# Attention and two mixture-of-experts layers on one core: closer choice steps, two lists in line, turns in two pieces, tile-by-tile reuse, early rows from 36 tiles

## The chip, the cores and the metric

The kernel runs on one core of a Trainium2 chip. The metric is the device time of one execution in microseconds. Times are given in us throughout. The core's engines are named as the profile names them: PE (TensorE, matrix products), PEld (its weight loads), DVE (VectorE), ACT (ScalarE), POOL (GpSimd) and SP (SyncE, which here issues transfers and runs no arithmetic).

## The reference

Three steps follow one another, each on the output of the one before:

```python
# 1 attention, B=8 batches, H=8 heads, S=576 positions, 64 per head
ret = (0.125 * q @ k.T * Dmat) @ v            # Dmat[i,j] = gamma_h**(i-j) for i>=j, else 0
x = ret as 4608 rows of 512
# 2 first mixture: each row goes to its best of 8 experts
e = argmax(x @ w_gate);  gate = softmax(x @ w_gate)[e]
x = gate * (relu(x @ w1[e]) @ w2[e])          # w1: 512x1024, w2: 1024x512
# 3 second mixture: greedy, each expert takes at most 576 rows
logits = x @ w_gate2
for (row, e) in order of falling logits:
    if row is free and e holds under 576 rows: assigned[row] = e
out = relu(x @ w1b[assigned]) @ w2b[assigned]
```

## The kernel before

**Attention** handles 36 tiles of 128 rows. For each tile a row of stages runs (list `stages`, in `step`), each some steps off the others. The stage `split` makes the gate's two f16 halves of the transposed row tile: ACT rounds `xT` to `xTh`, and POOL subtracts (`xTl = xT - xTh`, 128x512). PE multiplies both with the gate weights. Near the end of attention, some tiles of rows that are already stored in DRAM (`Xs`) are gathered by POOL for the first expert.

**The first mixture (moe1)** runs its experts e = 0 to 7 one after another. Every f32 product is made of three f16 products (high by high, high by low, low by high). An expert has a first layer (PE line L568 into PSUM `ph`; ACT makes `hh` from it at L573, DVE `hl` at L574) and a second layer (L590, L594 into `py`). Weights arrive in f32 `stage` buffers by SP transfers (L428), ACT rounds them (L449) and DVE takes the difference (L452). The rows of the next experts are gathered by POOL (L485), scaled by ACT and DVE and turned by transposing transfers of SP (L526, into `xT`). Where in a layer's groups of matmuls these side jobs are emitted is written out by hand in dictionaries `steps` and `at`, whose keys count matmul groups: `N6` gives the places in e6's first layer at which parts of e7's rows are prepared. Expert 0 starts with SA = 3 row tiles, and the first layer for its last two is run later, with side jobs at its own `steps`. The output rows of moe1 are written to `X1s`, 40 tiles of slots (8 experts by 5 tiles): tiles 30 to 39 are those of e6 and e7. In e6's first layer `fill` (places 124, 134, ...) writes tiles of it by indirect transfers of POOL (L1054) to listed positions; the last `LATE` tiles are written by plain SP transfers.

**The second mixture (moe2)** takes one expert after another, in eight phases. For each phase `choose` finds which expert is next, which rows it takes and their list. It searches a threshold in R = 5 digits; a digit has the steps `cnt` (DVE compares the keys, `cmp`, L1502; PE counts, L1508), `any` (DVE L1511, L1513; PE L1516) and `dig` (DVE L1520; PE L1523; DVE L1526), and after the digits come `sum` (PE L1540) and the list: `base` (PE L1603) and `list` (PE L629, then DVE up to the indices `ix`, L638). In phases 0, 1 and 7 the list runs in line, right after `sum`; in phases 2 to 6 it is put in a queue `aside` and runs beside the next choice's digits. When the list is there, `prepare` puts jobs in a queue `tasks`: gathers of five row tiles by POOL (L485, `xg`), their transposes by SP (L526), and the weights' loads and splits.

The moe2 loop is paced by PE: `during` counts the columns of the matmuls emitted, at 2.4 GHz, in ns. When the counter `left` is used up, the next step of the choice is emitted; its length for each kind of step is in `FIRST` (choice 0), `SECOND` (choice 1) and `PACE` (from choice 2 on). `ASIDE` is the same for lists in the queue, and `GAP` for the tasks (2.7 us up to phase 1, then 3.8 us). Each engine then executes its instructions in the order emitted. Choice p+1 and its list thus run in the layers of phase p. On POOL, the gathers stand in line with indirect writes of the output (L1697). On SP, the weight loads stand in line with the transposes and with a load of the chosen expert's number (`es`, L1723).

Tiles come from pools: `fp`, `wp2`, `sp` and the PSUM pool `fps` are opened after attention (`open_ffn`), in the memory that attention's pools held. In their plain form, a tile's first use waits for all that used the earlier pool's memory.

Of the kernel before, what the change touches and what calls it, by code (L numbers as in the profile page):

```python
# [24 lines left out]
SA = 3  # L25
LEAD_IN = 6
CAST = (4, 3)
EARLY = ((28, 1), (29, 0), (29, 1), (30, 1), (32, 0), (32, 1), (33, 0), (33, 1), (34, 0), (34, 1), (35, 0))
LOADS_LAST = 29
T0 = (76, 88)  # L30
LATE = 3
SOON = 3
P0 = (1, 12, 24, 70, 84)
RANK = (32, 40, 48)
N1 = (14, 82, 102, 122, 142, 170)
LOGITS = (96, 99, 101, 105, 109)
N6 = (10, 50, 66, 82, 98, 114)
G6 = (4, 8, 40, 122, 139)
G7 = (30, 36, 70, 106, 140, 170)
R = 5  # L40
NONE = -1.0e30
LEAD = 2
PACE = dict(key=7000, cnt=3300, any=2200, dig=1900, sum=3600, base=4000, list=3000)
SECOND = dict(key=3600, cnt=2500, any=1700, dig=1500, sum=2600, base=3000, list=2600)
FIRST = dict(key=3000, cnt=1700, any=1200, dig=800, sum=1900, base=3400, list=2600)
ASIDE = dict(key=8500, base=5000, list=5000)
AFTER_FIRST = 7500
GAP = (2700, 3800)

# [84 lines left out]
def attention(k, q, kk_, v, wg1, consts, X, after, ahead):  # L134
    tc = k.tc
# [196 lines left out]
    def step(s, stages):  # L332
        if s == 2 - LEAD_IN:
            nc.sync.dma_start(G[:, 0], consts[:, NC:NC + 512].rearrange("p (h q) -> p h q", q=128))
            k.wg1 = split_gate(k, wg1, "wg1", True)
        for f, off in stages[1:] + stages[:1] if s == LOADS_LAST else stages:
            if f is None:
                store()
                if (s, off) in EARLY:
                    next(ahead, None)  # L340
            elif 0 <= s - off < NT:
                f(D[s - off])
        for g, at0, every in after:
            if s >= at0 and (s - at0) % every == 0:
                next(g, None)
# [125 lines left out]
def open_ffn(k):  # L471
    tc = k.tc
    k.fctx = ExitStack()
    k.fp = k.fctx.enter_context(tc.tile_pool(name="fp", bufs=2))
    k.wp2 = k.fctx.enter_context(tc.tile_pool(name="wp2", bufs=1))
    k.sp = k.fctx.enter_context(tc.tile_pool(name="sp", bufs=1))
    k.fps = k.fctx.enter_context(tc.tile_pool(name="fps", bufs=2, space=bass.MemoryType.PSUM))
    k.tp = lambda shape: k.fps.tile(shape, F32, name="tp")


# [477 lines left out]
def moe1(k, X, X1, w1, w2):  # L958
# [106 lines left out]
    for e in range(8):  # L1065
# [77 lines left out]
        if e < 6:  # L1143
            x1 = columns(e)
            for s in (4, 0, 1, 2, 3) if small(e) else range(5):
                at = {8: load}
                if s == SA and e == 0:
                    steps = {64: load, 40: lambda: next(p1, None)}
                    mixed(layer1(k, xTs[0], w, CAP1, to=hs[0], spans=[[(128 * SA, CAP1 - 128 * SA)]]), steps)
                if s == (3 if small(e) else 4) and e < 6:  # L1150
                    ahead = prep(e + 2)
                    at[4] = lambda: next(ahead, None)
                if s == 4 and small(e):
                    last = tail(e, mixed(layer2(k, hs[e], w, s, True), at), x1)
                    next(last)
                    continue
                if s == 0 and small(e):
                    at[12] = partial(next, last)
                if e == 0 and s < SA:
                    go = lambda: next(p1, None)  # L1160
                    at = ({4: load, 12: go, 18: load}, {4: load, 18: load}, {2: go, 14: go, 21: load})[s]
                if e == 0 and s >= SA:
                    at = {2: go, 12: load, **({6: at[4]} if 4 in at else {})}
                if e == 5 and s < 2:
                    at[18] = load
                last = second(e, s, mixed(layer2(k, hs[e], w, s), at), x1)
# [311 lines left out]
def choose(k, ph, es_out, ix_out, aside):  # L1478
# [84 lines left out]
        late(nc.vector.tensor_scalar(z[:, 0], f.rem, 0.0, -30000.0, op0=OP.is_le, op1=OP.mult))  # L1563
        late(nc.vector.tensor_tensor(f.nr, z[:, 0], f.rem, op=OP.subtract))

    if ph in (0, 1, 7):
        yield from listed(k, ph, z, z1, key, s8, ix_out)
        if ph < 7:
            onward()
    else:  # L1570
        onward()
        aside.append(listed(k, ph, z, z1, key, s8, ix_out))
# [128 lines left out]
def moe2(k, X1, w1, w2, out, rest):  # L1701
# [18 lines left out]
    def choices():  # L1720

        for ph in range(8):
            for t in choose(k, ph, lambda es: ev.setdefault(ph, nc.sync.value_load(es[0:1, 0:1], min_val=0, max_val=7)),  # L1723
                            lambda ix, ph=ph: lx.setdefault(ph, ix), aside):
                while t == "sum" and aside:
                    side()
                if t == "key":
                    state.side = ASIDE[t]
                yield AFTER_FIRST if ph == 1 and t == "key" else (FIRST, SECOND, PACE)[min(ph, 2)][t]

    choice = choices()

# [32 lines left out]
    def prepare():  # L1765

        n = state.ph + 1
        if n == 0:
            if 0 in ev and 0 not in weights:
                half(0, 1)  # L1770
        elif n in lx and n not in weights:
            half(n, 1)
            t = tasks[-5:]
            del tasks[-5:]
            r = [(True, partial(turned, n, s)) for s in range(5)]
            tasks.extend([(True, partial(fetched, n))] + t[:2] + r[:2] + t[2:3] + r[2:4] + t[3:4] + r[4:] + t[4:])
            half(n, 2)

    def due(first):
# [130 lines left out]
```

## Time and profile before

| | us |
|---|---|
| median of 3 runs (lowest, highest) | 1115.98 (1108.40, 1120.48) |
| the profiled execution, and its span | 1111.99, 1110.2 |
| PE busy | 1027.6 |
| DVE busy | 615.2 |
| ACT busy | 431.3 |
| POOL busy | 303.3 |
| attention | 0 to 205 |
| moe1 | 205 to 653 |
| moe2 phases 0 to 7 | 653 to 1110 |

The engines run unsynchronized, each through its own list; an engine's idle time before an instruction is put down to what released it. PE is the engine to watch, as it is busy for nearly the whole span: its idle times, and the stretches in which its granted clock is below 1.0 (full speed is 2.4 GHz), are where time can be had. In rows of a timeline the first number is the start in us, the second the length, then engine, line and operation, `out<-in`, shape and count; brackets hold the idle time before the instruction and its releaser.

### The profile page before, as it was taken

The numbers are of one execution on the slowest core, as the hardware profiler recorded it, in microseconds if no ns is written. First come the engines' busy times: TensorE is split into PE (matmuls) and PEld (weight loads), VectorE is DVE, ScalarE is ACT, GpSimd is POOL, SyncE is SP. The second block draws the span as 40 slices with busy tenths as digits, with TensorE's granted clock in tenths as the row PEclk, the third lists the DMA queues.
The fourth block names the chain that finished last, engine by engine and source line by source line (L and its number), as shares of the span: only waits on it lengthen the run. The fifth ranks groups of instructions, "written<-read, shape, count | busy, mean of one in ns | idle before, by whom it ended". The sixth has DMA issues, their size and how long they took to land.

```text
span 1110.2 us, 23634 instructions
## 1 busy us (share of the span) xinstructions
PE 1027.6 (93%) x9227; PEld 680.3 (61%) x9227; DVE 615.2 (55%) x1678; ACT 431.3 (39%) x817; POOL 303.3 (27%) x542
## 2 busy tenths in 40 slices
PE   7999998798999999999899989995968989799996
PEld 5887887456766757474675446653636565557572
DVE  3455565786866666475625756643636473625140
ACT  3445545365645545364521342312313131324230
POOL 5444444221230313120311232213040313224101
PEclk9999999999999999999999999997998999899999
DMA  9999996488777887889750444628264555567521
GB/s 193 210 226 237 232 233 162 134 228 197 199 206 162 213 175 192 171 214 243 156 96 21 145 129 119 168 76 190 77 127 121 144 145 122 170 156 182 141 65 43
DMA packets 307255, 178.17 MB, mean 160 GB/s; under 512 B 240448, under 2 KB 273984, under 8 KB 307136
## 3 DMA queue, kind: packets, MB, share of 16 engines
q1 hardware_dynamic: 296672, 144.25, 56.2%
q0 software_dynamic: 10464, 32.34, 9.4%
q8 instruction: 74, 1.21, 0.5%
q14 instruction: 45, 0.37, 0.1%
HBM read 117.09 MB, written 31.28 MB: 134 GB/s over the span
## 4 chain that ended last, share of the span: by engine, by line
PE 73%; DMA 8%; issue 6%; DVE 4%; SPq 3%; ACT 3%; POOL 2%; POOLq 0%; ACTq 0%; DVEq 0%
PE ph L568 30%; PE py L594 24%; PE tp L120 7%; PE pO L120 5%; PE pS L120 3%; PE py L590 2%; SPq L526 2%; DMA xg<-X1s,ix 1%; POOL xg L485 1%; DMA xT<-xg 1%; DMA X1s<-x1r 1%; SPq L120 1%; DMA xg<-Xs,ix 1%; DMA xT<-xhl 1%; DMA out_dram<-x1r,ti 1%
## 5 line engine op out<-in xcount | busy, mean ns | idle before, releaser
L568 PE MATMUL ph<-xT,w1h 128*128 128x288 f16 (+4 forms) x2048 | 367.4, 295 | 44.3 <-DMA xT<-xg 31.6
L568 PEld LDWEIGHTS <-w1h 128*128 128x128 f16 x2048 | 198.3, 99 | 109.0 <-issue 31.2
L568 PE MATMUL ph<-xT,w1l 128*128 128x288 f16 (+4 forms) x1024 | 230.0, 295 | 0.0
L594 PE MATMUL py<-w2h,hh 128*128 128x512 f16 x512 | 194.3, 379 | 0.0
L594 PE MATMUL py<-w2h,hl 128*128 128x512 f16 x512 | 194.2, 379 | 0.0
L594 PE MATMUL py<-w2l,hh 128*128 128x512 f16 x512 | 194.1, 379 | 0.0
L594 PEld LDWEIGHTS <-hh 128*128 128x128 f16 x1024 | 98.2, 98 | 109.1 <-issue 0.8
L573 ACT ACTIVATE hh<-ph 128x576 f16<-128x576 f32 (+4 forms) x136 | 81.9, 604 | 188.2 <-PE ph L568 181.7
L574 DVE SCALAR_TENSOR_TENSOR hl<-ph,hh 128x576 f16<-128x576 f32 (+4 forms) x136 | 95.0, 699 | 57.4 <-ACT hh L573 56.7
L568 PEld LDWEIGHTS <-w1l 128*128 128x128 f16 x1024 | 100.8, 99 | 30.5 <-issue 1.0
L452 DVE SCALAR_TENSOR_TENSOR w1l<-stage,w1h 128x1024 f16<-128x1024 f32 x60 | 72.8, 1222 | 61.5 <-ACT w1h L449 60.5
L594 PEld LDWEIGHTS <-hl 128*128 128x128 f16 x512 | 50.1, 98 | 56.9
L452 DVE SCALAR_TENSOR_TENSOR w2l<-stage,w2h 128x1024 f16<-128x1024 f32 x64 | 78.1, 1224 | 9.6 <-ACT w2h L449 8.5
L120 DVE TENSOR_TENSOR s<-pS,ct 128x512 f32<-128x512 f32 x72 | 46.3, 685 | 42.6 <-PE pS L120 42.6
L449 ACT ACTIVATE w1h<-stage 128x1024 f16<-128x1024 f32 x60 | 61.8, 1047 | 19.1 <-DMA stage<-in_moe_w_dram 19.1
L449 ACT ACTIVATE w2h<-stage 128x1024 f16<-128x1024 f32 x64 | 66.9, 1047 | 2.2 <-DMA stage<-in_moe_w_dram 2.2
L120 POOL TENSOR_TENSOR xTl<-xT,xTh 128x512 f16<-128x512 f32 x35 | 42.6, 1218 | 87.3 <-ACT xTh L120 87.3
L499 ACT ACTIVATE x1r<-py 128x512 bf16<-128x512 f32 x37 | 22.1, 596 | 97.0 <-PE py L594 78.1
L485 POOL DMA_INDIRECT xg<-X1s,ix x40 | 42.2, 1055 | 59.9 <-DVE ix L638 20.9
L1697 POOL DMA_INDIRECT out_dram<-w2T,ti x20 | 20.6, 1032 | 138.0 <-ACT w2T L1696 114.0
L1697 POOL DMA_INDIRECT out_dram<-x1r,ti x20 | 22.8, 1141 | 124.5 <-ACT x1r L1696 105.0
L485 POOL DMA_INDIRECT xg<-Xs,ix x37 | 42.9, 1160 | 39.0 <-DVE ix L638 25.7
(391 smaller groups left out, 1461.3 us busy)
## 6 DMA issues: line engine op xcount, KB each, us to landing
stage<-in_moe_w_dram SPq DMA_DIRECT2D x128, 512.0 KB, 4.5
k<-in_k_dram SPq DMA_DIRECT2D x32, 256.0 KB, 5.5
q<-in_q_dram SPq DMA_DIRECT2D x32, 256.0 KB, 5.2
v<-in_v_dram SPq DMA_DIRECT2D x32, 256.0 KB, 5.0
X1s<-x1r SPq DMA_DIRECT2D x30, 257.0 KB, 3.5
Xs<-xr SPq DMA_DIRECT2D x6, 1028.0 KB, 7.2
Xs<-xr SPq DMA_DIRECT2D x3, 771.0 KB, 5.8
k<-in_k_dram SPq DMA_DIRECT2D x8, 128.0 KB, 6.5
```

What stands on the lines that cost most here:

```text
L120: return lambda *args, **kw: self.tc.keep_in_program_order(f(*args, **kw))
L449: d = nc.scalar.activation(at(h, i), t, AF.Copy, scale=128.0)
L452: d = nc.vector.scalar_tensor_tensor(at(l, i), t, 128.0, at(h, i), op0=OP.mult, op1=OP.subtract)
L485: nc.gpsimd.indirect_dma_start(out=xg[:M], out_offset=None, in_=src, in_offset=bass.IndirectOffsetOnAxis(ap=gidx[:M], axis=0))
L499: d = nc.scalar.activation(q.bitcast(mybir.dt.bfloat16), x, AF.Square, accum_out=sc[:, 0:1])
L526: nc.sync.dma_start(xT[:, :, S], x[:M], transpose=True)
L568: pe(k, nc.tensor.matmul(ph[:, z, :b], x[:, c, F], xT[:, y + c, a:a + b], start=i == 0, stop=i == 11))
L573: nc.scalar.activation(oh, src, AF.Relu)
L574: nc.vector.scalar_tensor_tensor(ol, src, 0.0, oh, op0=OP.max, op1=OP.subtract)
L590: pe(k, nc.tensor.matmul(py[64 * z:64 * z + 64, 0:256], x[:, f, S], y[:, f, 256 * z:256 * z + 256], start=i == 0, stop=i == 23))
L594: pe(k, nc.tensor.matmul(py, x[:, f, S], y[:, f, :], start=i == 0, stop=i == 23))
L1697: nc.gpsimd.indirect_dma_start(out=out2 if tail else out, out_offset=bass.IndirectOffsetOnAxis(ap=ti, axis=0), in_=y, in_offset=None)
```

## The change

1. `AT_GATHER = 30`: for token tile 30, `split`'s subtraction of `xTl` is made by DVE; POOL's goes.
2. `LATE` from 3 to 4: the rows that phase 0 gathers early come from tiles 0 to 35 of `X1s` (before: to 36). Tile 36 is written by an SP transfer like 37 to 39; `fill` is called 6 times in e6's layer, and the last indirect write by POOL comes one tile of the second layer earlier.
3. `N6`: from the second to the last, the places in e6's first layer at which parts of e7's rows are prepared are 18 groups later.
4. Paces: `PACE` cnt, any, dig and sum are 100 to 300 ns shorter. `SECOND` (key 400 ns longer) holds for choices 1 and 2. `ASIDE` is 1 to 1.5 us shorter. The list of phase 2 runs in line.
5. The pools `fp`, `wp2`, `sp` and `fps` have `reuse_waits="tile"`: a tile's first use waits for what used the memory it overlaps.
6. Expert 0's second part: other places for loads and for parts of e1's rows.
7. The five transposes of a phase are emitted as a group of three and a group of two, instead of five tasks.

```diff
-LATE = 3
+LATE = 4
+AT_GATHER = 30
-N6 = (10, 50, 66, 82, 98, 114)
+N6 = (10, 68, 84, 100, 116, 132)
-PACE = dict(key=7000, cnt=3300, any=2200, dig=1900, sum=3600, base=4000, list=3000)
-SECOND = dict(key=3600, cnt=2500, any=1700, dig=1500, sum=2600, base=3000, list=2600)
+PACE = dict(key=7000, cnt=3000, any=2000, dig=1800, sum=3300, base=4000, list=3000)
+SECOND = dict(key=4000, cnt=2500, any=1700, dig=1500, sum=2600, base=3000, list=2600)
-ASIDE = dict(key=8500, base=5000, list=5000)
+ASIDE = dict(key=7500, base=3500, list=4000)
...
-                f(D[s - off])
+                d = D[s - off]
+                f(d, nc.vector) if f is split and d.t == AT_GATHER else f(d)
...
-    k.fp = k.fctx.enter_context(tc.tile_pool(name="fp", bufs=2))
+    k.fp = k.fctx.enter_context(tc.tile_pool(name="fp", bufs=2, reuse_waits="tile"))
...
-                    steps = {64: load, 40: lambda: next(p1, None)}
+                    steps = {40: load, 20: lambda: next(p1, None), 60: lambda: next(p1, None)}
...
-                    at = {2: go, 12: load, **({6: at[4]} if 4 in at else {})}
+                    at = {2: go, 12: load} if s == SA else {4: at[4], 8: load}
...
-    if ph in (0, 1, 7):
+    if ph in (0, 1, 2, 7):
         yield from listed(k, ph, z, z1, key, s8, ix_out)
...
-                yield AFTER_FIRST if ph == 1 and t == "key" else (FIRST, SECOND, PACE)[min(ph, 2)][t]
+                yield AFTER_FIRST if ph == 1 and t == "key" else (FIRST, SECOND, SECOND, PACE)[min(ph, 3)][t]
...
-            tasks.extend([(True, partial(fetched, n))] + t[:2] + r[:2] + t[2:3] + r[2:4] + t[3:4] + r[4:] + t[4:])
+            pair = lambda *fs: (True, lambda: [f() for _, f in fs])
+            tasks.extend([(True, partial(fetched, n))] + t[:2] + [pair(*r[:3])] + t[2:3] + [pair(*r[3:])] + t[3:])
```

Line numbers of the changed kernel are one higher from line 30 on, and two higher from line 343 on: its L570 is L568 of before, and so on.

PE, before, where the first list matmuls of phase 2 stand (`py` is phase 1's second layer, `G` and `V` the list's tables):

```order
L594 LDWEIGHTS hh_9889
L594 MATMUL py_10361<-w2l_9910,hh_9889 128x512
L594 LDWEIGHTS hl_9890
L594 MATMUL py_10361<-w2h_9909,hl_9890 128x512
L629 LDWEIGHTS G_10328
L629 MATMUL tp_10377<-V_10276,G_10328 128x44 [waits Pool_49]
L629 LDWEIGHTS G_10328
L629 MATMUL tp_10377<-nV_10329,G_10328 128x44
```

PE, of the changed kernel, the same list:

```order
L570 LDWEIGHTS w1h_9662
L570 MATMUL ph_10142<-xT_9615,w1h_9662 128x288
L570 LDWEIGHTS w1h_9662
L570 MATMUL ph_10142<-xT_9615,w1h_9662 128x288
L631 LDWEIGHTS G_10123 [waits DVE_49]
L631 MATMUL tp_10153<-V_10085,G_10123 128x44 [waits Pool_49]
L631 LDWEIGHTS G_10123 [waits DVE_49]
L631 MATMUL tp_10153<-nV_10124,G_10123 128x44
```

The list has moved from phase 1's second layer to its first: before, 168 rows of PE lie between its first matmul and the first matmul of phase 2's first layer, and now 500.

POOL, before, at the gathers of phase 2 (L1697 writes phase 1's output rows; `V` belongs to the list):

```order
L1697 DMA out_dram<-x1r,ti 9216x256
L1611 CAST V<-ct 128x1
L1612 MEMSET V 128x2
L1697 DMA out_dram<-w2T,ti 4608x512
L1697 DMA out_dram<-x1r,ti 4608x512
L1697 DMA out_dram<-w2T,ti 4608x512
L485 DMA xg<-X1s,ix 128x514 x5
```

POOL, of the changed kernel, the same place:

```order
L1699 DMA out_dram<-x1r,ti 9216x256
L1613 CAST V<-ct 128x1
L1614 MEMSET V 128x2
L487 DMA xg<-X1s,ix 128x514 x5
```

The gathers now stand ahead of the three output writes of phase 1. At phase 3's gathers the three writes between `V` and the gathers go in the same way.

SP, before, the last loads of a phase's second-layer weights (128x2x512), the next choice's `es`, and the first load of the next phase's first layer (128x4x256):

```order
L428 DMA stage<-in_moe_w_dram 128x2x512
L428 ISA
L428 DMA stage<-in_moe_w_dram 128x2x512
L1723 TENSOR_LOAD es
L1723 ISA x2
L428 ISA
L428 DMA stage<-in_moe_w_dram 128x4x256
```

SP, of the changed kernel, the same place:

```order
L430 DMA stage<-in_moe_w_dram 128x2x512
L1725 TENSOR_LOAD es
L1725 ISA x2
L430 ISA
L430 DMA stage<-in_moe_w_dram 128x2x512
L430 ISA
L430 DMA stage<-in_moe_w_dram 128x4x256
```

The load of `es` has moved ahead of the last of the four second-layer loads (in the later phases ahead of more of them).

## Rows read from the trace of the kernel before

**Rows 1.** The page: the busy time of PE, its share of the span and its instructions.

```profile
PE 1027.6 (93%) x9227; PEld 680.3 (61%) x9227; DVE 615.2 (55%) x1678; ACT 431.3 (39%) x817; POOL 303.3 (27%) x542
```

**Rows 2.** Waits of PE: line, what it waited for, us in total, times, longest.

```profile
PE ph L568 <- DMA xT<-xg: 31.6, 7, 12.4
...
PE ph L568 <- DVE hl L574: 4.6, 4, 3.9
PE tp L1603 <- DVE fnr L1564: 3.4, 1, 3.4
PE ph L568 <- DVE sc L373: 3.2, 2, 3.0
PE tp L120 <- POOL xTl L120: 3.0, 1, 3.0
PE tp L530 <- DMA xg<-X1s,ix: 2.8, 2, 1.5
PE ph L568 <- DMA xT<-xhl: 2.5, 1, 2.5
...
PE tp L1508 <- DVE cmp L1502: 1.6, 1, 1.6
```

**Rows 3.** Windows: busy us of PE, PEld, DVE, ACT, POOL (instructions), PE clock, DMA share, GB/s.

```profile
653.00:705.00 52.00, 51.70 (x403) 30.96 (x403) 33.29 (x97) 18.28 (x32) 14.39 (x30) 1.00 0.53 140
...
705.00:757.00 52.00, 51.95 (x406) 32.61 (x402) 29.99 (x88) 14.09 (x19) 10.47 (x12) 1.00 0.31 100
...
771.00:774.00 3.00, 3.00 (x14) 1.83 (x13) 0.00 (x0) 0.00 (x0) 0.36 (x3) 0.52 1.05 395
...
183.00:186.00 3.00, 3.00 (x24) 2.49 (x22) 1.48 (x4) 0.72 (x4) 2.69 (x3) 0.56 0.13 51
...
214.00:217.00 3.00, 2.78 (x9) 1.35 (x10) 2.83 (x9) 0.90 (x1) 2.67 (x3) 0.52 0.39 100
...
541.00:545.00 4.00, 4.00 (x47) 2.64 (x46) 2.49 (x6) 1.54 (x3) 1.62 (x3) 0.60 1.12 144
```

**Rows 4.** Timeline of PE in moe2: lists of phases 2, 3, first products.

```profile
749.34 0.18 PE L629 MATMUL tp<-V,G 128*128 128x44 f16 x1
...
769.64 0.40 PE L568 MATMUL ph<-xT,w1h 128*128 128x288 f16 x1 [12.41 <-DMA xT<-xg]
...
811.96 0.18 PE L629 MATMUL tp<-V,G 128*128 128x44 f16 x1
...
832.16 0.40 PE L568 MATMUL ph<-xT,w1h 128*128 128x288 f16 x1 [8.84 <-DMA xT<-xg]
835.63 0.90 PE L568 MATMUL ph<-xT,w1h 128*128 128x288 f16 x3 [3.07 <-DMA xT<-xg]
```

**Rows 5.** Timeline of POOL at phase 3's gathers.

```profile
815.46 0.97 POOL L1697 DMA_INDIRECT out_dram<-x1r,ti  x1 [5.13 <-ACT x1r L1696]
```

**Rows 6.** Timeline of SP, the transposes of phase 3.

```profile
820.13 10.15 SPq L526 DMA_TRANSPOSE xT<-xg  x4
```

**Rows 7.** Timeline of DVE in phase 2, steps of choice 4.

```profile
819.18 0.15 DVE L1520 TENSOR_SCALAR_CACHE_REDUCE c<-tp 16x8 f32<-16x8 f32 x1 [1.81 <-PE tp L1517]
...
821.07 0.82 DVE L1502 TENSOR_TENSOR cmp<-key,thf 128x640 f16<-128x640 f32 x1
821.81 1.24 DVE L452 SCALAR_TENSOR_TENSOR w1l<-stage,w1h 128x1024 f16<-128x1024 f32 x1
```

**Rows 8.** Timeline of POOL and DVE at the end of attention.

```profile
181.42 1.17 POOL L120 TENSOR_TENSOR xTl<-xT,xTh 128x512 f16<-128x512 f32 x1
...
203.78 0.69 DVE L120 TENSOR_TENSOR xTl<-xT,xTh 128x512 f16<-128x512 f32 x1 [0.49 <-ACT xTh L120]
```

**Rows 9.** Timeline of DVE and ACT in expert 0's first layer.

```profile
211.30 0.17 DVE L638 TENSOR_SCALAR ix<-lw 128x2 int32<-128x2 f32 x1
...
213.08 0.87 ACT L573 ACTIVATE hh<-ph 128x384 f16<-128x384 f32 x2 [5.54 <-DMA Xs<-xr]
```

**Rows 10.** Timeline of POOL at phase 0's gathers.

```profile
643.59 0.98 POOL L485 DMA_INDIRECT xg<-X1s,ix  x1 [4.49 <-DMA X1s<-x1r,to]
```

More of the change, by code (lines that the diff above doesn't have):

```diff
@@ L473, in open_ffn @@
     k.fctx = ExitStack()
-    k.fp = k.fctx.enter_context(tc.tile_pool(name="fp", bufs=2))
-    k.wp2 = k.fctx.enter_context(tc.tile_pool(name="wp2", bufs=1))
-    k.sp = k.fctx.enter_context(tc.tile_pool(name="sp", bufs=1))
-    k.fps = k.fctx.enter_context(tc.tile_pool(name="fps", bufs=2, space=bass.MemoryType.PSUM))
+    k.fp = k.fctx.enter_context(tc.tile_pool(name="fp", bufs=2, reuse_waits="tile"))
+    k.wp2 = k.fctx.enter_context(tc.tile_pool(name="wp2", bufs=1, reuse_waits="tile"))
+    k.sp = k.fctx.enter_context(tc.tile_pool(name="sp", bufs=1, reuse_waits="tile"))
+    k.fps = k.fctx.enter_context(tc.tile_pool(name="fps", bufs=2, space=bass.MemoryType.PSUM, reuse_waits="tile"))
     k.tp = lambda shape: k.fps.tile(shape, F32, name="tp")
```

## The prediction

> **What bounds the kernel now.** I read the page's busy times first. PE is busy for 1027.6 us of the span, and no other engine for as much as 56% of it [rows 1], so the time comes from where PE waits, or runs at a lower clock. The list of PE's waits says which producers it waited for [rows 2]. The windows give the clock around these waits [rows 3], and the timelines what stands in the queue of the engine that was late [rows 4 to 10].
>
> The waits are few and large. The seven on the turned rows of moe2 (`xT<-xg`) come to 31.6 us [rows 2]; the reader is to see that they end the first products of a phase, each after a list that came too late: phase 2's list matmuls start at 749.34 and its first product at 769.64, after 12.41 us of idle PE [rows 4]. Behind a long wait PE also runs at the lower of its two levels: the 3 us from 771 show a granted clock of 0.52, while the 52 us before the wait show 1.00 [rows 3]. Such a stretch loses its length times (1 - clock): 3 x 0.48 = 1.4 us.
>
> **The change part by part.** The sum is made against the profiled execution, 1112.0 us, which is 4.0 us under the median of the three.
>
> *Lists earlier (parts 4 and 7).* The counted columns between a list's first matmul and its phase's first product, at 2.4 GHz, go from 8.9 to 34.2 us in phase 2, from 12.4 to 24.7 in phase 3, from 15.7 to 30.5 in phase 4 and from 19.1 to 36.8 in phase 5 (estimates by the two orders). In the trace phase 3's PE ran out of work 832.16 - 8.84 - 811.96 = 11.4 us behind its list [rows 4], 1 us less than counted; so I take 1 us off each. What has to fit in: list to first product 20.3 us in phase 2, and in phase 3 20.2 us to the first and 23.7 us to the second piece (835.63 - 811.96) [rows 4]. Phases 2, 4 and 5 then have 6 to 12 us to spare. Phase 3 has 23.7 us for 23.7, to the microsecond; but in its old chain an output write stood ahead of the gathers that had waited 5.13 us for ACT and held POOL until 816.4 [rows 5], and that write is behind the gathers now, which gives 1.0 us back. I take all seven waits as gone: 31.6. A clock loss goes with each of the four phases' waits; at 1.4 us each, the one that has its row [rows 3], 5.6. Together 37.2. Phase 1 is the comparison: its list is in line already and has 24.5 counted us, and the window in which its rows are gathered shows PE busy for 51.70 of 52 us [rows 3].
> The single wait of 3.4 us on `fnr` [rows 2] stays: in both orders phase 6's sum, base and list stand back to back on PE.
>
> *The two transposes tasks.* They add no instruction; a group of three goes to SP one `GAP` after the tasks ahead. In phase 3 four transposes held SP's queue from 820.13 for 10.15 us [rows 6], one behind the other, so the queue and not the emission set their pace. Nothing taken.
>
> *AT_GATHER.* PE waited 3.0 us once for POOL's `xTl` [rows 2], which stood behind three gathers and ran at 181.42 for 1.17 us; the same subtraction on DVE took 0.69 us [rows 8]. The stretch behind it ran at 0.56 for 3 us, a loss of 1.3 [rows 3]. All of it would be 4.3; what DVE's `s` loses is 0.7 at most. ACT is held by the same gathers (its square of a gathered tile waits for the transfer), so the next tile's gate products will wait for ACT instead. Bounds 0 and 4.3, taken 2.5, since the clock loss probably goes while a part of the wait returns.
> The Trainium skill (SBUF — State Buffer, section SBUF: two separate sides) says that a DVE operation with two SBUF inputs and a GpSimd operation that reads SBUF lock each other out for a whole instruction. `xTl` is such an operation, and by the rule it could wait for a gather's 0.95 us, leaving 1.6 of the 2.5. The trace does not show the lock here: the DVE split with two SBUF inputs that ran at 821.81, in the middle of phase 3's five gathers, took 1.24 us [rows 7], as long as such splits take on the average.
>
> *Reuse tile by tile.* In expert 0's first layer ACT's `hh` waited 5.54 us for the store `Xs<-xr` [rows 9], which it does not read: it is the pool-wide wait. DVE's `hl` follows it, and PE waits 3.9 us for that [rows 2], and then ran 3 us at 0.52, 1.4 lost [rows 3]. With the wait gone DVE is next: it is busy with the list until 211.30 + 0.17 = 211.5 [rows 9], and the first `hl` takes half of 1 us. PE then resumes at 212.1 instead of 214.2. That is 2.1, and 1.4 if the shorter stall leaves the clock alone: 3.5 (bounds 0 and 5.3).
>
> *Expert 0's second part.* e1's last transpose moves ahead, which is to end PE's one wait of 2.5 us on `xT<-xhl` [rows 2]. I take 2.0, for ACT and DVE get the jobs in a denser layer (bounds 0 and 2.5).
>
> *N6.* In e6 PE waited 3.0 us of 3.2 for `sc` [rows 2] because ACT's first square for e7 stood ahead of `hh` while its gathered rows were still in flight; then 4 us at 0.60 lost 1.6 [rows 3]. The jobs are 18 groups later now, well behind the gathers' landing. Some small waits of ACT's sequence stay, 1.2 us: 4.6 - 1.2 = 3.4 (bounds 0 and 4.6).
>
> *LATE.* Phase 0's gathers start at 643.59, having waited 4.49 us for the last indirect write into `X1s` [rows 10]; PE waits 2.8 us in two pieces for the rows [rows 2]. The last write is now one tile (some 5 us of PE) earlier, more than 4.49, so the gathers start that much earlier and the 2.8 us go (bounds 0 and 2.8).
>
> *What the closer steps cost.* A choice's step goes DVE, PE, DVE. In phase 2 DVE was idle for 1.81 us before a step's reduction because it waited for PE [rows 7]; steps 0.1 to 0.3 us closer leave more than 1 us of that. Choice 1 ran at the paces that choice 2 gets, and PE was busy for 51.70 of 52 us beside it [rows 3]. On SP the load of `es` now holds some weight loads until DVE has the sum; before, PE ran 51.95 of 52 us busy with a DMA share of 0.31 [rows 3], so there is room. For small waits I add 1.0 (bounds 0 and the rival below).
>
> Sum: 37.2 + 2.5 + 3.5 + 2.0 + 3.4 + 2.8 - 1.0 = 50.4, so 1112.0 - 50.4 = 1061.6 in a run like the profiled one. Against the median it would be 1066; against the lowest of the three 1058. I forecast 1062.
>
> **The rivals.**
> *Rows still late (chance 0.20).* The gathers and transposes now run beside other weight loads; 10.15 us for four transposes [rows 6] shows how loaded the transfers are. If the chain takes 6 us longer than in phase 3's trace, phase 3 waits 6 us and loses the clock's 1.4, and phase 4 is at its edge; if half of the 37.2 stays, it is 18.6. That gives 1069 to 1080. Against it: phase 1 had the same loads and no wait [rows 3].
> *Only the lists gain (0.13).* ACT and DVE are in fact the bound in attention's end and in moe1, and each small edit gives way to the next wait. Then 14.2 of the sum is missing: 1061.6 + 14.2 = 1076.
> *The change doesn't move what is late (0.02).* The list could be held by DVE's arithmetic and not by where it is emitted; then lists come when they did: 1100 to 1112. Against it: DVE waits for PE between steps [rows 7].
> *Closer steps stall PE (0.05), the slower side.* Each of the 16 steps of choices 2 to 7, 96 in all, could have PE wait for DVE's comparison. At the shortest paces, choice 0's, one such wait of 1.6 us is there [rows 2]. The gain of 51.4 without my 1.0 is eaten from 51.4 / 96 = 0.54 us a step on. If each step waits for a whole comparison, 0.82 us [rows 7], it is 78.7: 1112.0 - 51.4 + 78.7 = 1139. Against it are DVE's 1.81 us of idle time before a step.
>
> **How the numbers follow.** The forecast's own range is 1050 to 1068: the small edits' upper bounds together add 7.2 to the gain, the lower ones of two of them take some 6. Its chance is 0.56, and 0.04 goes to a still larger gain. Reaching up to the two cases beside it, the range is 1050 to 1080, which leaves out 0.04 below, 0.07 above and a part of the first two rivals. About 1% is what a measurement of this kernel can tell from no change (1105 to 1127): faster has the forecast, the larger gain, the first two rivals and a little of the third, 0.93, from which I take 0.03 for mechanisms I have not seen: 0.90. The same 0.05, slower 0.05.
>
> **What would show it right or wrong.** Right: no wait on `xT<-xg` over 2 us in moe2 and a clock of 1.00 throughout phases 2 to 5; phase 3's list matmuls some 12 us earlier against its first product; no 3 us wait on `xTl`; `hh` in expert 0 without a wait on `Xs<-xr`, and PE there idle for under 2 us; no wait on `xT<-xhl`; phase 0's gathers some 5 us earlier against their turns. The wait on `fnr` is still there, in phase 4's second layer. Wrong: waits of PE on `cmp`, `r`, `thf` or on weight loads in moe2 of more than 5 us together; a wait on `xT<-xg` in phase 3 over 5 us.

## The result, and the profile after

The changed kernel took 1071.7 us (median of 4 runs, 1069.69 to 1072.21), the kernel before, run beside it, 1117.9 us. The ratio is 0.9598, with a 95% interval of 0.9538 to 0.9658: about 46 us less. The forecast of 1062 us was 10 us too low; the time lies inside the stated range. The profiled execution took 1069.69 us with a span of 1067.9, 42.3 less than that of before.

PE's busy time on the page, to be read against [rows 1]:

```profile
PE 1016.8 (95%) x9227; PEld 673.6 (63%) x9227; DVE 617.8 (58%) x1679; ACT 429.9 (40%) x817; POOL 308.3 (29%) x539
```

PE has the same matmuls and is busy for 10.8 us less. In the kernel before it was busy for 28.2 us in stretches with a granted clock of 0.5, in the changed kernel for 10.5: at half the rate that is 8.8 us of the 10.8, and most of the rest is the start of the program (last section). The largest waits of PE in the changed kernel (line, what it waited for, us in total, times, longest), against [rows 2]:

```profile
PE tp L121 <- DMA k<-in_k_dram: 9.0, 3, 6.7
PE ph L570 <- DVE hl L576: 6.1, 5, 2.6
PE pO L121 <- DVE s L121: 4.8, 7, 1.2
PE tp L1605 <- DVE fnr L1566: 3.4, 1, 3.4
PE ph L570 <- DMA xT<-xhl: 2.9, 1, 2.9
PE tp L1519 <- DVE nm L376: 2.0, 1, 2.0
...
```

The first line is the start of the program; before, it was 7.9 us. The 31.6 us on `xT<-xg` are gone without a rest. The wait on `fnr` stayed, as expected. One has changed its place: `xT<-xhl` was 2.5 us in expert 1 and is 2.9 us in e7. The 2.0 us on `nm` are new.

Cut into the same pieces of work, the two traces read as follows (boundaries are the first products of layers; each line is the difference of two windows, rounded at the end):

| piece | before | after | gained | forecast |
|---|---|---|---|---|
| start and attention | 205.7 | 201.6 | 4.1 | 2.5 |
| expert 0 | 61.9 | 60.5 | 1.4 | 3.5, and the next line |
| expert 1 | 51.3 | 48.7 | 2.6 | 2.0 |
| experts 2 to 5 | 204.6 | 205.1 | -0.5 | 0 |
| first layers of e6, e7 | 64.2 | 65.0 | -0.9 | 3.4 |
| second layers of e6, e7 | 65.3 | 66.0 | -0.6 | 2.8 |
| phase 0 | 52.7 | 54.1 | -1.5 | 0 |
| phases 1 to 5 | 299.7 | 262.4 | 37.4 | 37.2 - 1.0 |
| phases 6, 7 | 104.8 | 104.6 | 0.2 | 0 |

Phase 0 takes 54.1 us in the run with the lists alone too, and 52.7 with the small edits alone (both below): its 1.5 us belong to the lists, which so gain 37.4 - 1.5 = 35.9 us.

Phases 1 to 3 of the kernel before, by windows (columns as in [rows 3]):

```profile
705.70:769.60 63.90, 51.47 (x394) 32.11 (x393) 33.72 (x90) 17.51 (x23) 16.11 (x26) 0.93 0.48 122
769.60:832.20 62.60, 52.90 (x396) 32.93 (x396) 30.60 (x85) 15.03 (x20) 14.17 (x24) 0.94 0.48 118
832.20:888.70 56.50, 52.96 (x392) 32.67 (x393) 28.69 (x83) 14.02 (x19) 12.19 (x23) 0.94 0.47 135
```

The same phases of the changed kernel:

```profile
701.00:754.00 53.00, 51.47 (x392) 32.06 (x391) 35.72 (x89) 18.81 (x24) 16.14 (x25) 1.00 0.62 179
754.00:805.40 51.40, 51.40 (x401) 32.23 (x399) 27.46 (x85) 12.20 (x17) 12.90 (x23) 1.00 0.50 114
805.40:856.50 51.10, 51.10 (x395) 32.13 (x394) 32.99 (x90) 15.98 (x21) 16.00 (x24) 1.00 0.66 160
```

Phases 2 and 3 are now busy PE from end to end at the full clock. A phase is 51.1 to 51.4 us, and with these matmuls there is no idle time left in it.

Phase 3, for which I had counted no more than 1.0 us to spare, has its list, its gathers, its last transpose and its first product here (PE, POOL, SP and PE; start, length, idle before and releaser in brackets):

```profile
780.91 0.18 PE L631 MATMUL tp<-V,G 128*128 128x44 f16 x1
783.32 1.00 POOL L487 DMA_INDIRECT xg<-X1s,ix  x1 [26.27 <-DVE ix L640]
797.74 2.11 SPq L528 DMA_TRANSPOSE xT<-xg  x1
805.35 0.66 PE L570 MATMUL ph<-xT,w1h 128*128 128x288 f16 x4
```

The gathers start 2.4 us behind the list, where it was 816.74 - 811.96 = 4.8 us with the output write ahead of them [rows 5]. A row of SP is the issue of a transfer, not its landing. By the semaphores in the two traces the fifth transpose had landed at 803.41, 20.1 us behind the first gather; before, it had landed at 835.58, 18.8 us behind it. So from the list to the last landing it is 22.5 us, where it was 23.6, and the product that needs the fifth transpose stands at 805.49: 2.1 us to spare.

### The profile page after: what moved, and what is told of

Same layout as the page of the kernel before. It is cut to its first block, busy times and chain, and to the rows that moved or that the text cites. A ratio compares the mean times of both kernels' runs of the same rounds, so it can differ in the third digit from the quotient of the medians.

```text
span 1067.9 us, 23627 instructions
## 1 busy us (share of the span) xinstructions
PE 1016.8 (95%) x9227; PEld 673.6 (63%) x9227; DVE 617.8 (58%) x1679; ACT 429.9 (40%) x817; POOL 308.3 (29%) x539
## 4 chain that ended last, share of the span: by engine, by line
PE 80%; DVE 7%; DMA 4%; issue 3%; ACT 3%; POOL 2%; SPq 1%; POOLq 0%; ACTq 0%; DVEq 0%
PE ph L570 32%; PE py L596 29%; PE tp L121 7%; PE pO L121 4%; PE pS L121 3%; PE py L592 2%; DMA X1s<-x1r 1%; POOL xg L487 1%; DMA xg<-Xs,ix 1%; SPq L121 1%; DMA stage<-in_moe_w_dram 1%; DVE hl L576 1%; DVE w1l L454 1%; DVE s L121 0%; PE tp L1510 0%
## 5 line engine op out<-in xcount | busy, mean ns | idle before, releaser
L570 PE MATMUL ph<-xT,w1h 128*128 128x288 f16 (+4 forms) x2048 | 359.8, 291 | 9.9 <-DVE hl L576 6.1
L570 PEld LDWEIGHTS <-w1h 128*128 128x128 f16 x2048 | 195.5, 98 | 71.9 <-issue 8.6
L570 PE MATMUL ph<-xT,w1l 128*128 128x288 f16 (+4 forms) x1024 | 226.6, 291 | 0.0
L570 PEld LDWEIGHTS <-w1l 128*128 128x128 f16 x1024 | 99.4, 98 | 30.8 <-issue 2.2
L501 ACT ACTIVATE x1r<-py 128x512 bf16<-128x512 f32 x37 | 22.1, 597 | 102.1 <-PE py L596 82.5
```

The costliest lines, as they stand in the source:

```text
L501: d = nc.scalar.activation(q.bitcast(mybir.dt.bfloat16), x, AF.Square, accum_out=sc[:, 0:1])
L570: pe(k, nc.tensor.matmul(ph[:, z, :b], x[:, c, F], xT[:, y + c, a:a + b], start=i == 0, stop=i == 11))
```

## The experiments

**Lists alone.** The kernel before with parts 4 and 7 (paces, list of phase 2 in line, transposes in two groups), nothing else.

```diff
-PACE = dict(key=7000, cnt=3300, any=2200, dig=1900, sum=3600, base=4000, list=3000)
+PACE = dict(key=7000, cnt=3000, any=2000, dig=1800, sum=3300, base=4000, list=3000)
...
-    if ph in (0, 1, 7):
+    if ph in (0, 1, 2, 7):
...
```

> The kernel before with parts 4 and 7 alone (paces, SECOND for choices 1 and 2, phase 2's list in line, ASIDE, transposes in two groups). Theory: these alone make the 37 us that moe2's phases 1 to 5 lost between the two traces, so about 1112 - 37 = 1075 us in a profiled run, no wait of PE on xT<-xg over 2 us, and the waits of before in attention, expert 0 and e6 still there (3.0 on xTl, 3.9 on hl, 3.0 on sc, 2.8 on xg). Rival: the rows come in time only because the small edits keep queues free ahead of moe2; then over 1085 us and waits on xT<-xg remain.

Measured: 1076.8 us against 1113.4 of before beside it, ratio 0.9662 (0.9631 to 0.9694): 36.6 us. Among its waits of PE:

```profile
PE ph L568 <- DVE sc L373: 5.0, 3, 2.9
...
PE tp L530 <- DMA xg<-X1s,ix: 3.5, 2, 2.1
...
PE ph L568 <- DVE hl L574: 3.3, 3, 2.7
PE tp L120 <- POOL xTl L120: 2.9, 1, 2.9
PE ph L568 <- DMA xT<-xhl: 2.4, 1, 2.4
```

There is no wait on `xT<-xg`, and the others of [rows 2] are all there, that on `hl` with 2.7 us at the longest instead of 3.9. Phases 1 to 5 take 262.2 us in this trace and 262.4 in the changed kernel's. The theory holds: parts 4 and 7 alone make the 37 us. What part 7, the grouped transposes, has in it was not run by itself.

**Small edits alone.** The changed kernel with parts 4 and 7 undone (the diff above, reversed).

> The changed kernel with parts 4 and 7 undone: the small edits alone. Theory, read from the two traces stage by stage: attention's end 2.4, expert 0 1.5 and e1 2.5 gained, the layers of e6 and e7 3.0 lost, so 3 us net, 1109 us, and moe2's 31.6 us of waits on xT<-xg as before. Rival, as the prediction had it: the small edits are worth 13 to 14 us when the lists don't disturb them: 1098 us.

Measured: 1103.5 us against 1113.4, ratio 0.9910 (0.9874 to 0.9946), 10 us, with 4 us of uncertainty either way. That is a gain of 6 to 14 us: the theory's 3 us lie outside it, the rival's 13 to 14 at its upper edge. PE's largest wait there:

```profile
PE ph L570 <- DMA xT<-xg: 27.5, 6, 10.3
```

The late lists are back, as they should be. The two halves add up: 36.6 and 9.9 make 46.5, and the whole change gained 46. The profiled span is 10.3 us shorter than that of before; 4.4 of it lie in start and attention, 2.6 each in expert 0 and expert 1.

**N6 a little earlier.**

```diff
-N6 = (10, 68, 84, 100, 116, 132)
+N6 = (10, 66, 80, 94, 108, 120)
```

> The changed kernel with N6 = (10, 66, 80, 94, 108, 120) for (10, 68, 84, 100, 116, 132). Theory: the last transpose of e7's rows stood behind two transposes of w2T on SP, since N6's last place (132) lies behind the gates' place 122; ahead of them again, PE's wait of 2.9 us on xT<-xhl and 1.7 us at the lower clock go: 4 to 4.6 us faster than the changed kernel. Rival: four transposes take 10.5 us and ACT's sequence is the bound: same within 1 us, with the wait moved to hl or sc.

What led to it is in SP's timeline of the changed kernel, transposes of e7's rows (`xT<-xhl`) and of the gates (`w2T`):

```profile
531.49 10.47 SPq L528 DMA_TRANSPOSE xT<-xhl  x4
542.06 1.26 SPq L693 DMA_TRANSPOSE w2T<-w2h  x1
543.38 1.31 SPq L693 DMA_TRANSPOSE w2T<-w2l  x1
544.78 1.68 SPq L528 DMA_TRANSPOSE xT<-xhl  x1
```

The fifth transpose of e7's rows came behind two others, 2.6 us, and PE waited 2.9 us for it. Measured with the new places: 1070.3 us, ratio 0.961 (0.9577 to 0.9643), the same as the changed kernel. PE's largest wait:

```profile
PE ph L570 <- DVE hl L576: 9.8, 8, 2.8
```

`xT<-xhl` is gone from the list, and `hl` has grown from 6.1 to 9.8. ACT's timeline in this run shows the way:

```profile
533.61 0.63 ACT L501 ACTIVATE xhl<-xg 128x512 bf16<-128x512 f32 x1 [2.17 <-DMA xT<-xhl]
```

ACT's square of a later row waits 2.17 us until an earlier row's transpose has read the `xhl` buffer that it writes; `hh` stands behind it, `hl` behind `hh`, and PE waits for `hl`. The rival holds: the wait goes from one engine to the next. SP issues the five transposes between 529.20 and 542.60; for 2.9 and for 3.0 us of these 13.4 us it waits until DVE has a row ready.

**Column operations of one output tile on DVE.** Output tile 36 only; POOL has them in the changed kernel.

```diff
-    nc.gpsimd.tensor_tensor(xr[:, 512:513], n[:, 2:3], sc[:, 0:1], op=OP.mult)
-    nc.gpsimd.tensor_copy(xr[:, 513:514], sc[:, 5:6])
+    eng = eng or nc.gpsimd
+    eng.tensor_tensor(xr[:, 512:513], n[:, 2:3], sc[:, 0:1], op=OP.mult)
+    eng.tensor_copy(xr[:, 513:514], sc[:, 5:6])
...
-        xr = out_rows(k, py, scales[e][s])
+        xr = out_rows(k, py, scales[e][s], nc.vector if e * 5 + s == NS - LATE else None)
```

> The changed kernel with the two column operations of output tile 36 on DVE instead of POOL. Theory: LATE = 4 made tile 36's store an SP transfer that needs two POOL operations, which stand behind the three gathers that LATE = 4 let start earlier; ACT's next output rows wait for that store (two buffers), DVE for ACT, and PE 2.0 us for DVE at 640, plus 1.7 us at the lower clock. Without POOL in that chain the store goes some 2.5 us earlier: 2 to 3.7 us faster, no wait at that place over 0.5 us. Rival: the store is late because the queue is loaded (weights, gathers): same, the wait stays.

The chain in the changed kernel, from its timeline of all engines:

```profile
633.19 0.96 POOL L487 DMA_INDIRECT xg<-X1s,ix  x1 [0.30 <-issue]
634.16 0.79 POOL L654 COPY x1r<-sc 128x1 f32<-128x1 f32 x1
634.92 0.18 POOL L653 TENSOR_TENSOR x1r<-nm,sc 128x1 f32<-128x1 f32 x1
635.12 0.34 SPq L1047 DMA_DIRECT2D X1s<-x1r  x1
```

and ACT behind it:

```profile
638.94 0.60 ACT L501 ACTIVATE x1r<-py 128x512 bf16<-128x512 f32 x1 [6.76 <-DMA X1s<-x1r]
```

The third gather, the two column operations and the store follow one another without a pause; ACT waits 6.76 us for the store, as the next output rows but one use the same buffer, and at 640.47 PE waits 2.0 us for DVE, whose `nm` waits for ACT. Measured: 1068.2 us, ratio 0.9595 (0.9561 to 0.9629). By the ratios that is level with the changed kernel, which did not run beside it; the profiled spans are 1064.4 and 1067.9. ACT in this run:

```profile
635.68 0.60 ACT L501 ACTIVATE x1r<-py 128x512 bf16<-128x512 f32 x1 [3.67 <-PE py L596]
```

It waits for PE now, not for a store, which SP issued at 627.40 instead of 635.12. The wait of PE on `nm` is gone, and so is the stretch at the lower clock behind it; a new wait of 1.7 us on `x1r` stands at 623. So the chain is shown. Its price is from the traces alone: of the 3.5 us between the spans 1.5 lie in attention, where this edit does nothing, and 2.6 from e6's second layer to the end of phase 0, less some tenths lost elsewhere.

**Phase 6's list in line.**

```diff
-    if ph in (0, 1, 2, 7):
+    if ph in (0, 1, 2, 6, 7):
```

> The changed kernel with phase 6's list in line as well (the list then has its own paced steps). Theory: the one wait that neither kernel touches, 3.4 us on fnr and 2.1 us on G at 905 in the changed kernel with 1.9 us at the lower clock behind it, comes from a list that is run through at once at the choice's sum; spaced out it goes: 6 to 7 us faster than the changed kernel, about 1064 us. Rival: DVE's chain behind the sum is that long whatever the pace, so PE waits in the next step: within 1.5 us of the changed kernel.

Measured: 1067.3 us, ratio 0.9593 (0.9559 to 0.9628). The waits on `fnr` and `G` at that place are gone; this one of PE is new:

```profile
920.63 0.17 PE L1542 MATMUL tp<-s,one_h 128*128 128x8 f16 x1 [3.57 <-DVE s L1539]
```

Choice 7 has no digits, so the arithmetic of its keys and its sum come in one step, and PE's matmul for the sum stands too early by these 3.6 us. From phase 4's second layer to the last phase, this trace is 4.4 us shorter than the changed kernel's. The rival holds in part: half of the stall moved to the next step.

**Tile 30's subtraction on POOL again.**

```diff
-AT_GATHER = 30
+AT_GATHER = 99
```

> The changed kernel without part 1 (tile 30's subtraction on POOL again). Theory: PE's wait of 3.0 us on xTl and 1.3 to 1.7 us at the lower clock come back, and the waits of 1.3 and 1.5 us on xT and scA that stand in the changed kernel at 181 and 188 go: 1.5 to 2.5 us slower. Rival: the later waits stay too, 4.3 us slower; or another engine was late in any case, same.

Measured: 1068.8 us, ratio 0.9618 (0.9593 to 0.9643), no slower; the wait on `xTl` did not come back. POOL's first gather at the end of attention in this run:

```profile
172.28 1.21 POOL L121 DMA_INDIRECT w2h<-Xs,ix  x1 [4.32 <-DVE s L121]
```

and in the changed kernel:

```profile
176.12 1.20 POOL L121 DMA_INDIRECT w2h<-Xs,ix  x1 [7.91 <-DMA k<-in_k_dram]
```

The gathers were 4 us earlier here. Tile 30's subtraction stood behind three of them, as in the kernel before, but with them it too came earlier:

```profile
176.01 1.18 POOL L121 TENSOR_TENSOR xTl<-xT,xTh 128x512 f16<-128x512 f32 x1
```

It ended at 177.19, and PE came to its product with it at 177.60. The first gather starts between 172 and 178 us over the profiled runs; in the late ones it was mostly a transfer that came last, in this one DVE's `s`, and SP issued the store of rows ahead of it (`Xs<-xr`) at 165.94 here and at 168.35 in the changed kernel. This run therefore does not price the edit. All kernels have a wait of PE of 1.18 us in mid-attention (it ends at 103.59 in before, at 101.93 in the changed kernel), and from its end to expert 0's first product the code is the same but for this edit and the pools. That takes 102.1 us without the edit and with late gathers (before, and lists alone: 203.82 - 101.72), 99.0 to 99.8 with it and gathers at 175 us or later (seven runs). With gathers at 172 to 173 us it takes 97.9 and 98.4 with the edit and 97.2 without it (this run). So the edit is worth 2.3 to 3.1 us when the gathers are late, and the one run with early gathers and without it shows no gain. The pools have no part in it: with them waiting as a whole (next run; gathers at 174.74) it is 99.0.

**Pools waiting as a whole again.**

```diff
-    k.fp = k.fctx.enter_context(tc.tile_pool(name="fp", bufs=2, reuse_waits="tile"))
+    k.fp = k.fctx.enter_context(tc.tile_pool(name="fp", bufs=2))
...
```

> The changed kernel without part 5 (pools wait as a whole). Theory: in expert 0's first layer hh waits 5 us for the store Xs<-xr again and PE 3.9 us for hl with 1.4 us at the lower clock, in place of the 2.0 us that it waits in the changed kernel: 2.5 to 3.5 us slower, all of it before 225 us. Rival: the tile-wise waits also free the tiles that moe2 uses later; then moe2 gets slower too and the sum is over 5 us.

Measured: 1069.9 us, ratio 0.9617 (0.9591 to 0.9643), too near to tell by medians. In the trace expert 0's first layer takes 22.2 us, against 19.2 in the changed kernel, with a PE wait of 3.0 us on `hl` and two stretches at the lower clock; 1.0 us of the 3.0 is given back before expert 1. The theory is right in place, and in size for this layer; in the sum it is no more than 2 us. A part of that is the clock: of the eleven profiled runs with the edit five take 19.2 us for this layer, and six, with a stretch at the lower clock in it, 19.7 to 20.9.

**Much closer steps.** `FIRST` in place of `PACE` for choices 3 to 7.

```diff
-(FIRST, SECOND, SECOND, PACE)[min(ph, 3)][t]
+(FIRST, SECOND, SECOND, FIRST)[min(ph, 3)][t]
```

> The changed kernel with the paces FIRST (cnt 1.7, any 1.2, dig 0.8 us) for choices 3 to 7 in place of PACE (3.0, 2.0, 1.8). It measures the rival of the prediction that closer steps make PE wait for DVE. Theory: a digit costs DVE and PE about 4 us of chain against the 3.7 us of the paces, so PE waits now, 0.3 to 0.5 us a step on 80 steps: 20 to 40 us of waits on cmp, s1s, r, c and thf, 1090 to 1110 us. Rival: DVE keeps up as in choice 0, which shows one wait of 1.6 us: 1072 to 1080 us.

Measured: 1079.8 us, ratio 0.9722 (0.9675 to 0.977): 8 us more than the changed kernel by the medians and by the profiled spans, 14 by the ratios, so that the rival's range holds and not the theory's. Among its waits of PE:

```profile
PE tp L1519 <- DVE r L1515: 5.5, 6, 2.2
PE tp L1510 <- DVE cmp L1504: 4.5, 2, 2.7
```

Phases 1 to 6 are 9 us longer together. Choice 7 has no digits, so the edit touches 65 steps, and that is 0.14 us a step, at paces little over half of those in use. The mechanism of the slower rival exists; even at these paces it is far from the 0.54 us a step at which it would have decided. (For the same reason the prediction's 96 steps are 81, and 51.4 / 81 = 0.63 us.)

**The changed kernel again, and three that build on it.** These four ran on one chip. First the changed kernel, unchanged.

> The changed kernel itself once more, beside the three below on one chip. It tells which of its waits and of its stretches at the lower clock repeat. Theory: the waits repeat within 0.3 us, but whether a wait of 2 to 3 us is followed by 1.7 us at the lower clock does not, and POOL's first gather at the end of attention (172 to 176 us so far) does not either: the profiled span lies within 4 us of 1067.9. Rival: all repeats, and the span is within 1 us.

Measured: 1071.8 us (1064.73 to 1074.44), span 1069.6, ratio 0.9596 (0.9529 to 0.9662). Behind the start of the program the waits of over 1 us repeat within 0.5 us, POOL's first gather stands at 176.13 again, and the span is 1.7 us longer. The stretches at the lower clock don't repeat: the last section has two of them.

> The changed kernel with phase 6's list in line, 6 us more before the sum of choice 7, and output tile 36's two column operations on DVE. Theory: phase 6's list in line left a wait of 3.6 us at the sum of choice 7, which has no digits, so that its keys and its sum came in one step; with more room that goes too, and with e4's 3 us the sum is 7.3 + 3 = 10 us less than the changed kernel, about 1060 us; no wait over 1 us between 860 and 960 us. Rival: the room moves the list of phase 7 so late that its rows are waited for, or the gain is under 5 us.

```diff
+    if ph in (0, 1, 2, 6, 7):
...
...
+                yield AFTER_FIRST if ph == 1 and t == "key" else (FIRST, SECOND, SECOND, PACE)[min(ph, 3)][t] + (6000 if ph == 7 and t == "sum" else 0)
```

The column operations are those of e4. Measured: 1058.1 us (1055.89 to 1061.51), ratio to before 0.9479 (0.9425 to 0.9533), 13.7 us under the changed kernel beside it by the medians and 9.9 us by the profiled runs. This is the best of all. From the first product of phase 1 to that of phase 5 it is one piece:

```profile
700.80:907.40 206.60, 204.69 (x1572) 128.38 (x1572) 129.20 (x354) 63.93 (x84) 61.06 (x99) 1.00 0.60 153
```

PE is idle for 1.9 us in 206.6 us, and the wait at the sum of choice 7 is gone as well.

> As f1, but the column operations of the output tiles of expert 5 and of tiles 30 and 36 on ACT instead of POOL (36: instead of DVE). Theory: POOL's gathers of e7's rows stood 6 us behind a column copy that waited for the store of an earlier output tile; now they start some 4 us earlier in e6's layer, and PE's waits of 1.0 and 2.9 us there shrink to under 1.5 us together: 2 to 4 us faster than f1. Rival: the five transposes of e7's rows (10 to 13 us on SP beside the gathers) are the bound and the waits stay: same as f1.

```diff
+    if eng:
+        nc.scalar.activation(xr[:, 512:513], n[:, 2:3], AF.Copy, scale=sc[:, 0:1])
+        nc.scalar.activation(xr[:, 513:514], sc[:, 5:6], AF.Copy)
...
+        xr = out_rows(k, py, scales[e][s], e == 5 or e * 5 + s in (30, NS - LATE))
...
```

Measured: 1069.9 us, 12 us slower than f1 by the medians and 8 by the profiled spans. ACT in e6's layer:

```profile
524.80 0.20 ACT L655 ACTIVATE x1r<-sc 128x1 f32<-128x1 f32 x1 [3.91 <-DMA X1s<-x1r]
...
533.11 0.63 ACT L501 ACTIVATE xhl<-xg 128x512 bf16<-128x512 f32 x1 [5.03 <-DMA xg<-Xs,ix]
```

The column copy waits for the store on ACT as it did on POOL, now with `hh` and the squares behind it; the gathers started at 526.98, later than f1's 524.51, not earlier. My theory was wrong: the wait is for the buffer, and on ACT more work stands behind it.

> As f2, with N6 = (10, 66, 80, 94, 108, 120) as in e3. Theory: with the gathers 4 us earlier the rows' arithmetic is no longer late at the earlier places, and the last transpose stands ahead of the gates' transposes: no wait over 1 us in e6's layer, 1 to 3 us faster than f2. Rival, as in e3: the wait moves to hl (2.8 us), same as f2 or slower.

Measured: 1070.1 us, with a single wait of 6.5 us on `hl`: the rival, as with e3.

## Why the prediction was right, and where not

**Lists.** Right in mechanism, and the sum is met: 36.2 us forecast (37.2 less the 1.0 of the closer steps), 35.9 in the traces, 36.6 by the runs with the lists alone. The places named held too: phases 2 to 5 at a clock of 1.00 but for the `fnr` stall, which stood in phase 4's second layer as said. That the sum fits so well is in part luck, as two sizes in it were off and cancel. PE was busy for 13.8 us at the lower clock behind the waits of phases 2 to 5, which is 6.9 us lost where I had booked 5.6. And the closer steps cost more than I took (next paragraph).

The rival of rows still late fell, with 2.1 us to spare in phase 3. I had booked 1.0 us for the output write that left POOL's queue, by its own length; its wait for ACT left with it, and the gathers start 2.4 us sooner behind the list, but 1.3 of that is lost again between the first gather and the last landing. My reading of [rows 6], that SP's queue set the transposes' pace, was wrong without a price: by the semaphores the first four gathers had landed at 820.07, 821.58, 823.26 and 826.83, and the four transposes start at 820.13, 821.60, 823.31 and 826.85. The gathers' landing set the pace.

**Closer steps.** I took 1.0 us for small waits. The changed kernel shows 0.8 and 0.7 us at choice 2's sum and base, which `SECOND` made closer, and 0.6 us on `r`; and phase 0 is 1.5 us longer, with 421 instructions of PE in its trace instead of 411. By what is missing, 31.6 + 6.9 - 35.9, the cost is 2.6 us: the size was too small.

**Reuse tile by tile.** Expert 0's first layer lost 2.8 us against 3.5. PE still waits 1.98 us there for `hl`, as forecast (1.8), because DVE has the list. Behind it 1.3 us is given back in expert 0's second part: PE waits 2.6 us for `hl` where it had been 1.4 for `nm`, since ACT's output rows wait 2.4 us for a store. The 1.4 us for the clock are no sure gain: six of eleven runs with this edit have a stretch at the lower clock in this layer (above).

**Expert 0's second part.** The wait on `xT<-xhl` went, as said: 2.6 us for 2.0, and it is still there with the lists alone.

**AT_GATHER.** Of the table's 4.1 us 2.4 are the edit's; 1.7 is the start of the program and has nothing to do with the change (last section). Forecast 2.5: right, with late gathers, which both profiled runs have. What came back, 1.3 and 1.5 us, is on DVE (`xT` and `scA`), not on ACT as I had it. That the gain hangs on when transfers land I had not seen. The lock between DVE and GpSimd that the Trainium skill (SBUF — State Buffer, section SBUF: two separate sides) tells of is not put to the test: with the column operations on DVE, for one, tile 30's subtraction ran at 170.88, ahead of the first gather at 172.29.

**N6.** Forecast 3.4, measured -0.9. The step that failed is "the jobs are 18 groups later now, well behind the gathers' landing": it looks at ACT and the landing alone. A moved job also has a transpose in SP's queue, and N6's last place went past the gates' place 122, so that two transposes stood ahead of it. The row was ready at 541.43, its transpose issued at 544.78 and landed at 548.64, when PE went on. E3 shows that the step would have failed without that too: rows, `xhl` buffers and transposes wait for one another, and PE then waits 2.8 us for `hl`. How much was lost depends on the clock: with the same `N6` and no stretch at the lower clock (e2 and e6) the two layers take 63.4 and 63.5 us, a gain of 0.7 to 0.8.

**LATE.** Forecast 2.8, measured -0.6 over the second layers of e6 and e7. The step "the gathers start that much earlier and the 2.8 us go" was right for itself: PE's wait on `xg` is gone. What is late next, I had not asked: three gathers now stand ahead of two column operations on POOL on which output tile 36's store waits, and since LATE = 4 makes that store an SP transfer of a buffer that ACT needs, PE pays 2.0 us and 1.7 us of clock.

**The sum.** The small edits came to 5 us in the profiled pair, without the start of the program, where 14.2 had been booked; the runs with them alone give 9.9 with an interval of 4 either way. N6 and LATE, for which 6.2 had been booked and which cost 1.5, are most of the difference. LATE and part 6 were not run by themselves; what is said of them is from the traces. The rival "only the lists gain", 1076 us, lay nearer to the result than the forecast did. I also placed the forecast by the profiled run, 4 us under the median. That the time still lies inside the range is owed to its upper end, which was set by the rivals. (The small edits' upper bounds add 5.3 us to the gain, 6.3 with the closer steps, and not 7.2.)

## What to carry to other kernels

A chain that is late by its place in the program, with an engine idle behind it, gains what the trace shows when it is moved, and the clock's loss behind the wait comes back with it. For an edit that relieves one queue, write down what stands behind the moved instruction on each queue that it enters or passes, and which buffer the next one up waits for: N6 and LATE removed their waits and got others of the same size. A wait of under 3 us in a pipeline of three engines may be a limit of another stage than the one at which it shows: in e3 it only went from `xT<-xhl` to `hl`.

## What the hardware showed unexpectedly

**The same wait of 2 to 3 us costs the clock in one run and not in another.** The same wait on `xT<-xhl` is followed in the changed kernel by this stretch (window; the PE clock is the third last number):

```profile
549.00:553.00 4.00, 4.00 (x19) 2.36 (x18) 0.00 (x0) 0.00 (x0) 0.97 (x1) 0.57 0.64 88
```

and with the small edits alone, behind 3.0 us of the same wait, by this one:

```profile
547.00:551.00 4.00, 3.94 (x42) 2.96 (x43) 0.04 (x1) 0.61 (x1) 0.97 (x1) 1.00 0.64 108
```

Of 2.4 GHz and 1.2 GHz the second has the full level throughout, the first mostly the lower one, and 1.7 us are lost. The changed kernel run again (f0) fell to the lower level at 202, behind waits of 0.5 us and less, and at 243, behind one of 2.2 us:

```profile
202.00:206.00 4.00, 4.00 (x18) 1.97 (x17) 3.72 (x27) 1.19 (x5) 0.55 (x4) 0.57 0.52 197
243.00:247.00 4.00, 3.79 (x20) 2.77 (x20) 3.06 (x12) 3.04 (x7) 0.64 (x4) 0.57 1.32 206
```

In its first run the same waits, and at 243 one of 2.6 us, had cost nothing:

```profile
202.00:206.00 4.00, 2.97 (x21) 1.70 (x20) 3.71 (x27) 1.18 (x5) 0.55 (x3) 1.00 0.52 197
243.00:247.00 4.00, 3.54 (x31) 3.02 (x31) 3.72 (x13) 3.91 (x10) 1.24 (x4) 1.00 1.08 226
```

What decides is not shown. Over the profiled runs of the changed kernel and its variants 3.5 to 8.8 us of busy time are lost at the lower clock. One kernel's times go with it: the four executions of f0 had spans of 1069.6, 1072.6, 1070.3 and 1062.9 us at a mean granted clock of 0.987, 0.986, 0.987 and 0.993, and span times (1 - clock) is 6.5 us less in the last than in the first, nearly the whole of its lead. The Trainium skill (TensorE: Matmul & The Clock Gate, section What's actually happening) says that the chip judges activity in windows of its own that do not start with the kernel; the runs agree in so far as the same wait, of 2.9 and of 3.0 us, had a clock of 0.57 and of 1.00 behind it.

**The start of the program differs by 1.7 us.** In the profiled run of before PE's matmuls were slow until 19 us, in the changed kernel's only until 13 us, though nothing there was changed. Before:

```profile
16.42 1.98 PE L120 MATMUL pO<-s,vf 128*64 128x128 f32 x16
```

After:

```profile
16.16 1.09 PE L121 MATMUL pO<-s,vf 128*64 128x128 f32 x16
```

The lead of 1.7 us in attention is there by 86 us, ahead of every edit. It is not the changed code: f3, which has all of it, started as slowly as the kernel before,

```profile
16.30 1.98 PE L121 MATMUL pO<-s,vf 128*64 128x128 f32 x16
```

and the lists alone, with attention as before, as fast as the changed kernel: the wait in mid-attention ends at 103.24 and 101.72 there.
